# The second layer with its operands exchanged: token parts stationary, 384 weight columns moving, and one accumulator bank handed to attention

## The chip, the cores and the metric

The kernel runs on one core of a Trainium2 chip. The metric is the device time of one execution in microseconds. Three runs of the kernel before took 716.56, 717.89 and 721.01 us, so the median is 717.89 us.

## The reference

The program computes a delta-rule linear attention over 4 batches, 8 heads, 768 steps and 48 dimensions per head, and puts its output through a dense two-layer network with a softplus between the layers, all in float32. (The code calls the network a MoE, but there is one expert and no routing.)

```python
for t in range(S):                               # S = 768, per batch and head
    y[:, :, t] = np.einsum('bhd,bhde->bhe', q[:, :, t], state)
    v_old = np.einsum('bhde,bhd->bhe', state, k_n[:, :, t])
    state = state + bt * np.einsum('bhd,bhe->bhde', k_n[:, :, t], vt - v_old)
...
h = x @ w_in                                     # 3072 tokens x 384  ->  2048
g = np.maximum(h, 0.0) + np.log1p(np.exp(-np.abs(h)))
return (g @ w_out).astype(np.float32)            # 3072 x 2048  ->  384
```

## The kernel before

Time is cut into 12 chunks of 64 steps. With 4 batches, a chunk is 256 tokens of the network. Attention runs chunk by chunk: `gram` forms the products of the keys, `invert` solves small triangular systems column by column on VectorE (lines 214 and 220, once for each pair of chunks), `cross`, `seq_a` and `seq_b` carry the state through the chunk (TensorE matmuls of 32 to 64 columns, with PSUM results copied out by ScalarE and VectorE). It writes the chunk's output `x` as two float32r parts, high and low.

The network works on a chunk's 256 tokens. `DFF` = 2048 hidden rows are 16 tiles `f` of 128, taken two at a time, so there are 12 x 8 = 96 groups. In a group:

- **First layer (L422)**: for each of the two `f`, 9 matmuls (3 row tiles times 3 terms of the high/low split) with the weights as the stationary operand (128x128) and 256 token columns moving, into the PSUM tile `ph`. That is 18 matmuls a group, 1728 in all.
- **Softplus**: ScalarE L426, L427, L428, VectorE L429, then VectorE L432 rounds to the high part `gh`, and GpSimd L433 makes the low part `gl`. `ph`, `a`, `gh` and `gl` have two buffers each.
- **Second layer (L406)**, in the inner function `outp`: for each `f`, 3 terms (high weights with `gh`, low weights with `gh`, high weights with `gl`) times 3 tiles `e` of 128 output columns. The weights are stationary and 256 tokens of `gh` or `gl` move. That is also 18 matmuls a group and 1728 in all. They accumulate over a whole chunk in `po`, a tile of three PSUM banks (one buffer), with the 384 outputs on partitions and the tokens along the row.

`outp` of a group is emitted after the first layer of the next group (`late`). At the end of a chunk ScalarE copies all of `po` to `ot` (L413) and SyncE stores it (L414); in the very last chunk the terms are sorted so that the three `gl` terms of each tile come last, and each 128-row tile is copied and stored by itself (L410, L411).

PSUM has eight banks: `ph` takes two, `po` three, and `ps_a`, which holds every PSUM tile of attention (`pa`), three.

Attention steps are emitted between network groups by `attend` with a target (`RATE`, `LEAD`, `FIRST`). Each engine then executes in a fixed order, which the framework's scheduler sets at build time; in the opening part the order of TensorE is written out by hand. Dependences are kept by tile: a matmul that writes one bank of `po` waits for an earlier copy that reads another bank of the same `po`.

Of the kernel before, what the change touches and what calls it, by code (L numbers as in the profile page):

```python
# [7 lines left out]
F32 = mybir.dt.float32  # L8
# [8 lines left out]
B, H, S, D = 4, 8, 768, 48  # L17
NT, DM, DFF = B * S, H * D, 2048
P = 128
C = 64                 # time steps per chunk  # L20
HB = 32                # half chunk
QB = 16                # quarter chunk
NS = S // C            # chunks
NP = B * H // 2        # head pairs, p = 4 * b + h // 2
NK = DM // P           # 128-row tiles of the model dimension
NF = DFF // P          # 128-row tiles of the hidden dimension
RATE, LEAD, FIRST = 1.15, 12, 3     # attention units per MoE group, their lead and head start
QW = C + D             # [Q^T | state] columns per pair
# Where a weight tile is staged: tiles that are not in use yet.
STAGE = "x2 x3 x1 w12 w13 w14 w15 x2 x3 x1 w12 w13 x2 x3 w15 x2".split()  # L30
N16 = 1                # pairs of chunks that are inverted from blocks of 16


@with_exitstack
def deltanet_moe(ctx, tc, kT, qT, kN, vN, beta, wts, out):
    nc = tc.nc
# [3 lines left out]
    two = E(tc.tile_pool(name="two", bufs=2))  # L40
    ps_h = E(tc.tile_pool(name="ps_h", bufs=2, space=PSUM))
    ps_o = E(tc.tile_pool(name="ps_o", bufs=1, space=PSUM))
    ps_a = E(tc.tile_pool(name="ps_a", bufs=3, space=PSUM))
    nc.scalar.preload_act_table_set("natural_log_exp_and_others")

# [1 line left out]
    # Of a pair of heads (a, b), a has its tokens on partitions 0-63 and its d rows on 64-111,  # L47
    # b its tokens on 64-127 and its d rows on 0-47.
    tk = [slice(ab * C, (ab + 1) * C) for ab in range(2)]
    lo = [slice(ab * C, ab * C + HB) for ab in range(2)]  # L50
    hi = [slice(ab * C + HB, (ab + 1) * C) for ab in range(2)]
# [2 lines left out]
    pad = [slice((1 - ab) * C + HB, (2 - ab) * C) for ab in range(2)]  # L54

    kts = [const.tile([P, NP, C], F32, name=f"kt{i}") for i in range(3)]
    # Per head and pair: [P^T | U] on the token rows, [Q^T | state] on the d rows.
    big = const.tile([P, 2 * NP * QW + 16], F32, name="big")
    bv = big[:, 0:2 * NP * QW].rearrange("p (h a c) -> p h a c", h=2, c=QW)
    # Per head and pair: K on the token rows, the identity on the d rows.  # L60
    ki = const.tile([P, 2, NP, D], F32, name="ki")
    Z = const.tile([P, HB, HB], F32, name="Z")
    maskL = const.tile([P, QB], F32, name="maskL")
# [114 lines left out]
            nc.scalar.copy(off[hi[ab]], pa[hi[ab]])  # L178

    def invert(u, cT, ncT):  # L180
        # Z = (1 + diag(c) L)^-1 diag(c) per block: row m starts from its diagonal, and each of its
        # columns j, once final, is carried to the columns before it.
        ltq = one.tile([P, HB, HB], F32, name="ltq")
        nc.vector.transpose(ltq.rearrange("p j i -> p i j"),
                            LTD[u].rearrange("p q i -> p i q"))
        n = QB if u < N16 else HB
        blocks = range(0, HB, n)
        for a in blocks:
            d = (slice(None), slice(a, a + n), slice(a, a + n))
            mask = nc.gpsimd.affine_select(  # L190
                out=Z[d], in_=ncT[:, a:a + n].unsqueeze(1).to_broadcast([P, n, n]),
                compare_op=ALU.is_gt, fill=0.0, base=0, pattern=[[1, n], [-1, n]],
                channel_multiplier=0)
            nc.vector.tensor_tensor(ltq[d], ltq[d], Z[d], op=ALU.mult)
            nc.vector.tensor_tensor(Z[d], ltq[d],
                                    cT[:, a:a + n].unsqueeze(2).to_broadcast([P, n, n]),
                                    op=ALU.mult)
        lds = []
        if u < N16:
            for j in range(2):  # L200
                ld = two.tile([P, NP, HB], F32, name="gh")
                nc.gpsimd.memset(ld[:, :, QB:], 0.0)
                nc.gpsimd.tensor_tensor(ld[:, :, 0:QB], LTD[u][:, j * NP:(j + 1) * NP, 0:QB],
                                        maskL.unsqueeze(1).to_broadcast([P, NP, QB]), op=ALU.mult)
                lds.append(ld)
        if u == 0:
            tmp = one.tile([P, HB, HB], F32, name="tx")
        else:
            tmp = one.tile([P, HB, HB], F32, name="work")
        nc.vector.tensor_copy(Z.rearrange("p a b -> p (a b)")[:, 0:HB * HB:HB + 1], cT)  # L210
        for j in range(n - 2, 0, -1):
            r = n - 1 - j
            for a in blocks:
                nc.vector.tensor_tensor(  # L214
                    tmp[:, a:a + r, 0:j],
                    Z[:, a + j + 1:a + n, a + j:a + j + 1].to_broadcast([P, r, j]),
                    ltq[:, a + j:a + j + 1, a:a + j].to_broadcast([P, r, j]), op=ALU.mult)
            for a in blocks:
                zj = Z[:, a + j + 1:a + n, a:a + j]
                nc.vector.tensor_tensor(zj, zj, tmp[:, a:a + r, 0:j], op=ALU.add)  # L220
        return mask, lds
# [6 lines left out]
                                   Z.rearrange("p c j -> p j c") if u < N16 else Z)  # L228

    def join(u, lds):  # L230
        # Blocks of 16 joined to blocks of 32: Z = D - D L D, D the inverted blocks of 16.
        td, tx = TD[u], TX[u]
        for j in range(2):
            w1 = two.tile([P, NP, QB], F32, name="gl")
# [127 lines left out]
            yield  # L362

    def weights(f):
        # float64 words to float32, then to float32r parts: 2^e (0 below float32's range) times
        # 1 + mantissa.
        st = one.tile([P, 4 * DM], I32, name=STAGE[f])
        nc.sync.dma_start(st, wts[f])
        words = st.rearrange("p (n w) -> p n w", w=2)
# [19 lines left out]
    def moe():  # L389
        n = B * C  # L390
        late = None
        for s in range(NS):
            xr = [[X[s][:, i, k].rearrange("p b t -> p (b t)") for k in range(NK)]
                  for i in range(2)]
            po = ps_o.tile([P, NK, 512], F32, name="po")

            def outp(f0, gh, gl, po=po, s=s):
                terms = [(f, i, e) for f in range(f0, f0 + 2) for i in range(3) for e in range(NK)]
                last = f0 + 2 == NF and s == NS - 1
                if last:  # L400
                    terms.sort(key=lambda t: (t[1] == 2, t[2]))
                if f0 + 2 == NF:
                    ot = two.tile([P, NK, n], F32, name="ex", bufs=3)
                for f, i, e in terms:
                    a, b = ((0, 0), (1, 0), (0, 1))[i]
                    nc.tensor.matmul(po[:, e, 0:n], W[f][:, a, DM + e * P:DM + (e + 1) * P],  # L406
                                     (gh, gl)[b][:, f - f0], start=(f == 0 and i == 0),
                                     stop=(f == NF - 1 and i == 2))
                    if last and f == NF - 1 and i == 2:
                        nc.scalar.copy(ot[:, e], po[:, e, 0:n])  # L410
                        nc.sync.dma_start(out[s, e], ot[:, e])  # L411
                if f0 + 2 == NF and not last:
                    nc.scalar.copy(ot, po[:, :, 0:n])  # L413
                    nc.sync.dma_start(out[s].rearrange("e p c -> p e c"), ot)  # L414

            for f0 in range(0, NF, 2):
                ph = ps_h.tile([P, 2, n], F32, name="ph")
# [104 lines left out]
            steps_done = s + 1  # L522

    def attend(steps, target):
        """Emits attention work, at least so many steps and up to a number of units."""
        nonlocal units
        while steps_done < NS and (steps_done < steps or units + 1 <= target):
            r = next(ag, None)
# [65 lines left out]
```

## Time and profile before

| | before |
|---|---|
| median of three runs | 717.89 us |
| span of the profiled execution | 718.2 us (the page gives no other time of it) |
| TensorE matmuls, busy | 633.2 us, 88% |
| TensorE weight loads, busy | 599.3 us, 83% |
| VectorE busy | 488.6 us, 68% |
| ScalarE busy | 365.7 us, 51% |
| GpSimd busy | 246.4 us, 34% |

How to read it: a matmul and its weight load are separate rows (PE and PEld) and overlap; a matmul's end is modelled, so the number that counts is the distance between the starts of two matmuls that follow each other. Plain float32 matmuls, as attention has them, appear as two records each, float32r ones, as the network has them, as one. The span stands 0.3 us above the median of the runs, so the profiled execution can be taken for a typical one.

### The profile page before, as it was taken

To read this page: it belongs to the slowest core of one execution; us is meant where nothing else is said; L and a number is where in the kernel's file an instruction comes from. 1 tells how busy PE (TensorE), PEld (TensorE's weight loads), DVE (VectorE), ACT (ScalarE), POOL (GpSimd) and SP (SyncE) were. 2 spreads that over 40 slices of the span, in tenths; PEclk is the share of its full clock that TensorE was granted. 3 is DMA by queue.
4 is the path that set the end of the run, shared out by engine and by line. 5 is a ranking of instruction groups with operands and counts; after the bars stand their busy time and mean duration, and the time that the engine had idled before them with its cause. 6 is when DMAs were issued, how large, how long until landed. Compare 5 with 4: busy or idle time off the path is not lost.

```text
span 718.2 us, 23130 instructions
## 1 busy us (share of the span) xinstructions
PE 633.2 (88%) x10176; PEld 599.3 (83%) x10176; DVE 488.6 (68%) x956; ACT 365.7 (51%) x667; POOL 246.4 (34%) x183
## 2 busy tenths in 40 slices
PE   4227566879999899998999999999999999999997
PEld 3226556778899799998899999999989999999997
DVE  3999999999789955699635998459992524222221
ACT  3537875465365344652445545456545454544443
POOL 5517776553241221521213323233222222232232
PEclk9999568899999999999999999999999999999999
DMA  9923431202213121220213111321202121000000
GB/s 229 321 77 98 112 116 42 67 24 57 68 47 79 46 57 50 65 56 24 60 42 92 47 35 46 79 69 36 68 24 57 46 38 43 2 13 23 1 23 23
DMA packets 36563, 44.83 MB, mean 62 GB/s; under 512 B 21616, under 2 KB 28656, under 8 KB 36464
## 3 DMA queue, kind: packets, MB, share of 16 engines
q1 hardware_dynamic: 36464, 43.36, 21.6%
q8 instruction: 80, 1.31, 0.8%
q14 instruction: 19, 0.16, 0.1%
HBM read 36.27 MB, written 4.72 MB: 57 GB/s over the span
## 4 chain that ended last, share of the span: by engine, by line
PE 50%; DVE 38%; issue 4%; DMA 3%; ACT 2%; POOL 2%; SPq 1%; DVEq 0%; POOLq 0%; ACTq 0%
PE po L406 21%; PE ph L422 19%; DVE Z L220 6%; DVE work L214 6%; DVE a L429 3%; PE pa L291 2%; DVE ex L378 2%; DVE ex L374 2%; DVE big L298 2%; DVE gh L432 2%; PE pa L336 2%; DMA x<-wts 2%; DVE big L295 2%; PE pa L324 1%; DVE x L383 1%
## 5 line engine op out<-in xcount | busy, mean ns | idle before, releaser
L422 PE MATMUL ph<-x,w 128*128 128x256 f32 x1728 | 238.8, 292 | 9.2 <-DVE a L429 7.2
L433 POOL TENSOR_TENSOR gl<-a,gh 128x512 fp32r<-128x512 f32 x96 | 128.0, 1334 | 345.5 <-DVE gh L432 297.2
L422 PEld LDWEIGHTS ph<-x,w 128*128 128x128 f32 x1728 | 222.7, 198 | 14.3 <-DVE a L429 7.7
L406 PE MATMUL po<-gh,w 128*128 128x256 f32 x1152 | 176.4, 290 | 8.2 <-DVE gh L432 6.8
L426 ACT ACTIVATE a<-ph 128x512 f32<-128x512 f32 x96 | 57.3, 597 | 216.4 <-PE ph L422 212.7
L429 DVE SCALAR_TENSOR_TENSOR a<-ph,a 128x512 f32<-128x512 f32 x96 | 66.0, 688 | 148.2 <-ACT a L428 147.7
L406 PEld LDWEIGHTS po<-gh,w 128*128 128x128 f32 x1152 | 152.5, 193 | 13.6 <-DVE gh L432 8.5
L406 PE MATMUL po<-gl,w 128*128 128x256 f32 x576 | 103.8, 289 | 3.8 <-POOL gl L433 2.2
L406 PEld LDWEIGHTS po<-gl,w 128*128 128x128 f32 x576 | 82.8, 192 | 7.9 <-POOL gl L433 5.4
L214 DVE TENSOR_TENSOR work<-Z,ltq 128x30 f32<-128x30 f32 (+9 forms) x150 | 64.4, 429 | 3.8
L220 DVE TENSOR_TENSOR Z<-Z,work 128x30 f32<-128x30 f32 (+9 forms) x150 | 63.9, 426 | 3.9
L427 ACT ACTIVATE a<-a 128x512 f32<-128x512 f32 x96 | 60.5, 630 | 2.9
L428 ACT ACTIVATE a<-a 128x512 f32<-128x512 f32 x96 | 60.6, 631 | 2.0
L432 DVE CAST gh<-a 128x512 fp32r<-128x512 f32 x96 | 47.9, 500 | 2.4
L295 DVE TENSOR_TENSOR big<-nv,pa 64x192 f32<-64x192 f32 x88 | 30.9, 351 | 18.3 <-PE pa L291 16.6
L291 PE MATMUL pa<-big,kt 48*64 48x112 f32 x704 | 41.6, 265 | 0.3 <-DVE big L298 0.3
L291 PEld LDWEIGHTS pa<-big,kt 48*64 48x64 f32 x704 | 35.0, 136 | 4.1 <-PE pa L291 0.5
L298 DVE TENSOR_TENSOR big<-pa,maskP 64x256 f32<-64x256 f32 x88 | 37.0, 421 | 1.4
L112 POOL TENSOR_TENSOR nv<-nv 128x768 f32<-128x768 f32 x10 | 15.3, 1526 | 43.4 <-DMA nv<-kN 43.4
L327 ACT COPY big<-pa 32x384 f32<-32x384 f32 x48 | 22.6, 471 | 11.1 <-PE pa L324 10.1
L336 PE MATMUL pa<-big 128*64 128x64 f32 x768 | 27.9, 230 | 0.2
L336 PEld LDWEIGHTS pa<-big 128*64 128x64 f32 x768 | 25.5, 143 | 2.6 <-ACT big L327 0.7
(103 smaller groups left out, 758.8 us busy)
## 6 DMA issues: line engine op xcount, KB each, us to landing
x<-wts SPq DMA_DIRECT2D x9, 768.0 KB, 4.4
w<-wts SPq DMA_DIRECT2D x7, 768.0 KB, 10.0
kt<-kT SPq DMA_DIRECT2D x24, 192.0 KB, 3.3
big<-qT SPq DMA_DIRECT2D x24, 192.0 KB, 4.0
ki<-kN SPq DMA_DIRECT2D x24, 192.0 KB, 3.3
nv<-vN SPq DMA_DIRECT2D x12, 384.0 KB, 3.1
nv<-kN SPq DMA_DIRECT2D x11, 384.0 KB, 3.1
out<-ex SPq DMA_DIRECT2D x11, 384.0 KB, 2.6
```

The source lines that it names most:

```text
L214: nc.vector.tensor_tensor(tmp[:, a:a + r, 0:j], Z[:, a + j + 1:a + n, a + j:a + j + 1].to_broadcast([P, r, j]), ltq[:, a + j:a + j + 1, a: ...
L220: nc.vector.tensor_tensor(zj, zj, tmp[:, a:a + r, 0:j], op=ALU.add)
L291: nc.tensor.matmul(pk[tk[ab], pp, :], kt[dr[ab], p, :], bv[dr[ab], ab, p, :], start=True, stop=True)
L336: nc.tensor.matmul(py[tk[ab], pp, :], big[:, at + C:at + 2 * C], big[:, at:at + C], start=True, stop=True)
L406: nc.tensor.matmul(po[:, e, 0:n], W[f][:, a, DM + e * P:DM + (e + 1) * P], (gh, gl)[b][:, f - f0], start=(f == 0 and i == 0), stop=(f == N ...
L422: nc.tensor.matmul(ph[:, f - f0], W[f][:, a, k * P:(k + 1) * P], xr[b][k], start=(c == 0), stop=(c == 3 * NK - 1))
L426: nc.scalar.activation(a, ph, AF.Abs)
L427: nc.scalar.activation(a, a, AF.Exp, scale=-1.0)
L428: nc.scalar.activation(a, a, AF.Ln, bias=1.0)
L429: nc.vector.scalar_tensor_tensor(a, ph, 0.0, a, op0=ALU.max, op1=ALU.add)
L432: nc.vector.tensor_copy(gh, a)
L433: nc.gpsimd.tensor_tensor(gl, a, gh, op=ALU.subtract)
```

## The change

Only the second layer is turned round. The 128-token slice of `gh` or `gl` is now the stationary operand, and all 384 output columns of the weights move. With two halves `h` of 128 tokens, a group has 2 x 3 x 2 = 12 matmuls of 384 columns in place of 18 of 256. `po` needs two banks in place of three, one for each half, and holds tokens on partitions and outputs along the row. The last group of every chunk sorts its terms by half, and each half is copied (128x384) and stored by itself: 24 copies and 24 stores in place of 11 + 3. The freed bank goes to `ps_a`, which gets four. The output array in memory has another shape to match. Comments were taken out too. The file lost four lines, so that L422 and L433 of before are L418 and L429 after the change, L406 becomes L405, L413 becomes L409.

```diff
-    ps_a = E(tc.tile_pool(name="ps_a", bufs=3, space=PSUM))
+    ps_a = E(tc.tile_pool(name="ps_a", bufs=4, space=PSUM))
...
-            po = ps_o.tile([P, NK, 512], F32, name="po")
+            po = ps_o.tile([P, 2, 512], F32, name="po")
 
             def outp(f0, gh, gl, po=po, s=s):
-                terms = [(f, i, e) for f in range(f0, f0 + 2) for i in range(3) for e in range(NK)]
-                last = f0 + 2 == NF and s == NS - 1
-                if last:
-                    terms.sort(key=lambda t: (t[1] == 2, t[2]))
+                terms = [(f, i, h) for f in range(f0, f0 + 2) for i in range(3) for h in range(2)]
                 if f0 + 2 == NF:
-                    ot = two.tile([P, NK, n], F32, name="ex", bufs=3)
-                for f, i, e in terms:
+                    terms.sort(key=lambda t: t[2])
+                    ot = two.tile([P, 2, DM], F32, name="ex", bufs=3)
+                for f, i, h in terms:
                     a, b = ((0, 0), (1, 0), (0, 1))[i]
-                    nc.tensor.matmul(po[:, e, 0:n], W[f][:, a, DM + e * P:DM + (e + 1) * P],
-                                     (gh, gl)[b][:, f - f0], start=(f == 0 and i == 0),
+                    nc.tensor.matmul(po[:, h, 0:DM], (gh, gl)[b][:, f - f0, h * P:(h + 1) * P],
+                                     W[f][:, a, DM:], start=(f == 0 and i == 0),
                                      stop=(f == NF - 1 and i == 2))
-                    if last and f == NF - 1 and i == 2:
-                        nc.scalar.copy(ot[:, e], po[:, e, 0:n])
-                        nc.sync.dma_start(out[s, e], ot[:, e])
-                if f0 + 2 == NF and not last:
-                    nc.scalar.copy(ot, po[:, :, 0:n])
-                    nc.sync.dma_start(out[s].rearrange("e p c -> p e c"), ot)
+                    if f == NF - 1 and i == 2:
+                        nc.scalar.copy(ot[:, h], po[:, h, 0:DM])
+                        nc.sync.dma_start(out[s, h], ot[:, h])
...
-    args.append(nc.dram_tensor("out", (NS, NK, P, B * C), F32, kind="ExternalOutput").ap())
+    args.append(nc.dram_tensor("out", (NS, 2, P, DM), F32, kind="ExternalOutput").ap())
```

The scheduler makes a new order from this on every engine. Three places on TensorE matter below. In their rows L406 and L422 are the second and the first layer before, L405 and L418 the same after the change.

**Place one, the end of the first network chunk.** Before, from the last first-layer matmuls that stand between the second layer's:

```order
L422 MATMUL ph<-x_1597,w_813 128x256 x4
L406 MATMUL po<-gh,w_967 128x256 x6
L422 MATMUL ph<-x_1597,w_813 128x256 x5
L406 MATMUL po<-gl,w_967 128x256 x3
L406 MATMUL po<-gh,w_981 128x256 x6
L406 MATMUL po<-gl,w_981 128x256 x3
L422 MATMUL ph<-x_1597,w_827 128x256 x9
L422 MATMUL ph<-x_1597,w_841 128x256 x9
```

After the change, the same place:

```order
L418 MATMUL ph<-x_1585,w_813 128x256 x7
L405 MATMUL po<-w_967,gh 128x384 x2
L418 MATMUL ph<-x_1585,w_813 128x256 x2
L405 MATMUL po<-w_967,gl 128x384
L405 MATMUL po<-w_981,gh 128x384 x2
L405 MATMUL po<-w_981,gl 128x384
L418 MATMUL ph<-x_1585,w_827 128x256 x9
L418 MATMUL ph<-x_1585,w_841 128x256 x9
L405 MATMUL po<-w_967,gh 128x384 x2
L405 MATMUL po<-w_967,gl 128x384
```

Before, the last group of the chunk (weights w_967 and w_981) is finished in one go, and a first-layer group follows. Now its first half is finished, a first-layer group (w_827, w_841) comes between, and then the second half, which has to wait for the copy of the first.

**Place two, a little later, where attention's `cross` (L261) and `seq_a` (L291) come.** Before:

```order
L261 MATMUL pa<-td,off 32x32 x32
L291 MATMUL pa<-big,kt_76 64x112 x16
L406 MATMUL po<-gh,w_799 128x256 x6
L422 MATMUL ph<-x_1597,w_855 128x256 x4
L291 MATMUL pa<-big,kt_76 64x112 x8
L406 MATMUL po<-gl,w_799 128x256
L291 MATMUL pa<-big,kt_76 64x112 x8
L406 MATMUL po<-gl,w_799 128x256 x2
L406 MATMUL po<-gh,w_813 128x256 x6
L406 MATMUL po<-gl,w_813 128x256 x3
```

After the change:

```order
L405 MATMUL po<-w_155,gh 128x384 x4
L405 MATMUL po<-w_155,gl 128x384 x2
L261 MATMUL pa<-td,off 32x32 x32
L291 MATMUL pa<-big,kt_76 64x112 x32
L405 MATMUL po<-w_799,gh 128x384 x4
L405 MATMUL po<-w_799,gl 128x384 x2
L405 MATMUL po<-w_813,gh 128x384 x4
L405 MATMUL po<-w_813,gl 128x384 x2
```

Before, `seq_a`'s 32 matmuls stand in three pieces between second-layer matmuls, and four first-layer ones stand among them. Now all 32, which fill four banks of `ps_a`, stand in one piece right behind `cross`, whose result holds one of the four.

**Place three, the end of the program.** Before, the last seven rows, of 48 second-layer matmuls that stand behind the last of L422:

```order
L406 MATMUL po<-gh,w_981 128x256 x2
L406 MATMUL po<-gl,w_967 128x256
L406 MATMUL po<-gl,w_981 128x256
L406 MATMUL po<-gl,w_967 128x256
L406 MATMUL po<-gl,w_981 128x256
L406 MATMUL po<-gl,w_967 128x256
L406 MATMUL po<-gl,w_981 128x256
```

After the change, all rows from the last first-layer matmuls on, without the last three:

```order
L418 MATMUL ph<-x_7970,w_981 128x256 x6
L405 MATMUL po<-w_939,gh 128x384 x4
L405 MATMUL po<-w_939,gl 128x384 x2
L405 MATMUL po<-w_953,gh 128x384 x4
L405 MATMUL po<-w_953,gl 128x384 x2
L405 MATMUL po<-w_967,gh 128x384 x2
L405 MATMUL po<-w_967,gl 128x384
L405 MATMUL po<-w_981,gh 128x384 x2
L405 MATMUL po<-w_981,gl 128x384
L405 MATMUL po<-w_967,gh 128x384 x2
```

Now 24 second-layer matmuls stand behind the last first-layer one. Of the last group's twelve, the third already needs `gl`; before, the twelve that need only `gh` all stood ahead of the six that need `gl`.

Over the whole program, TensorE changes between network and attention matmuls 211 times before and 233 times after the change.

More of the change, by code (lines that the diff above doesn't have):

```diff
@@ L591 @@
     r = _run(nc, [data], core_ids=[0])
-    o = r.results[0]["out"].reshape(NS, NK, P, B, C).transpose(3, 0, 4, 1, 2)
+    o = r.results[0]["out"].reshape(NS, B, C, DM).transpose(1, 0, 2, 3)
     return np.ascontiguousarray(o).reshape(NT, DM)
```

## The prediction

> **What bounds the kernel now.** I read the page first: the busy shares, the slices and the chain.
>
> ```profile
> PE 633.2 (88%) x10176; PEld 599.3 (83%) x10176; DVE 488.6 (68%) x956; ACT 365.7 (51%) x667; POOL 246.4 (34%) x183
> ...
> PE   4227566879999899998999999999999999999997
> ...
> DVE  3999999999789955699635998459992524222221
> ...
> PEclk9999568899999999999999999999999999999999
> ...
> PE 50%; DVE 38%; issue 4%; DMA 3%; ACT 2%; POOL 2%; SPq 1%; DVEq 0%; POOLq 0%; ACTq 0%
> ```
>
> A slice is 18 us. For the first nine or ten VectorE is full and TensorE is not; after that TensorE is full to the end, and VectorE comes back to nine tenths in some places. The chain says the same: half of it is TensorE, 38% VectorE. So I asked for stretches, cut where the inversions are (all engines first, then the second layer alone).
>
> ```profile
> core 0: us, PE busy (x) PEld busy (x) DVE busy (x) ACT busy (x) POOL busy (x), PEclk, DMA share, GB/s
> 107.00:171.00 64.00, 50.51 (x734) 45.93 (x733) 62.88 (x95) 35.17 (x58) 35.62 (x20) 0.88 0.16 47
> 208.00:251.00 43.00, 41.00 (x612) 38.02 (x612) 39.84 (x89) 20.98 (x40) 11.35 (x9) 1.00 0.20 52
> ...
> 485.00:528.00 43.00, 41.73 (x660) 39.18 (x658) 40.95 (x93) 22.73 (x46) 12.13 (x9) 1.00 0.16 43
> 528.00:634.00 106.00, 105.82 (x1550) 102.19 (x1551) 42.75 (x95) 52.23 (x100) 24.77 (x19) 1.00 0.15 37
> ```
>
> ```profile
> 0.00:171.00 171.00, 19.18 (x126) 17.05 (x126) 0.88 0.40 117
> 208.00:251.00 43.00, 15.64 (x112) 13.85 (x112) 1.00 0.20 52
> 302.00:346.00 44.00, 16.01 (x113) 14.11 (x114) 1.00 0.20 51
> 395.00:435.00 40.00, 15.71 (x113) 13.78 (x111) 1.00 0.17 47
> 485.00:528.00 43.00, 14.81 (x108) 13.39 (x108) 1.00 0.16 43
> ```
>
> There are three kinds of stretch. Up to 171 us VectorE sets the pace (62.88 of 64 us in the last part); 126 second-layer matmuls are there, 7 groups of 18. In four later stretches (the first and the last are shown) VectorE is at 93% (39.84 of 43) to 95% (40.95) and TensorE is not quite full; 112 + 113 + 113 + 108 = 446 matmuls, 24.8 groups. In the rest TensorE is as good as always busy (105.82 of 106): 1728 - 126 - 446 = 1156 matmuls, 64.2 groups. Only there is TensorE time certainly time of the kernel.
>
> **What one matmul of 384 columns costs.** The trace has none. It has 256 columns at full clock and at half the granted clock, here first-layer matmuls in rows without another's between (start, length of the row, count; the second row is from the stretch whose clock the third gives), and weight loads of several widths (mean ns behind the bar's first comma).
>
> ```profile
> 647.02 3.52 PE L422 MATMUL ph<-x,w 128*128 128x256 f32 x28
> ```
>
> ```profile
> 115.08 3.41 PE L422 MATMUL ph<-x,w 128*128 128x256 f32 x15
> ```
>
> ```profile
> 115.50:118.00 2.50, 2.50 (x13) 2.50 (x13) 0.50 0.03 7
> ```
>
> ```profile
> L422 PE MATMUL ph<-x,w x18: 323/415/420, 114.7 to 118.3; 128*128 128x256 f32 x18
> ```
>
> ```profile
> L422 PEld LDWEIGHTS ph<-x,w 128*128 128x128 f32 x1728 | 222.7, 198 | 14.3 <-DVE a L429 7.7 <-issue 1.6 <-DMA x<-x 1.3
> ...
> L149 PEld LDWEIGHTS pa<-kt 48*32 48x32 f32 x640 | 19.0, 110 | 8.1 <-issue 6.8 <-ACT off L155 0.2
> ```
>
> At half clock a matmul lasts 0.415 us, so the starts are (3.41 - 0.415) / 14 = 214 ns apart: 0.835 ns a column. At full clock they are (3.52 - 0.28) / 27 = 120 ns apart, with 0.28 for the last one's length (0.29 is the mean of L422 in the page's groups). Streaming at twice the half-clock rate would be 107 ns, so 13 of the 120 are something else. Loading 96 columns more takes 198 - 110 = 88 ns, 0.92 ns a column, so 128 stationary columns need about 117 ns beside a stream of 107. The load, I conclude, sets the 120, and at half clock, where the distance is twice 107 and no more, nothing stands on top of the stream. With 384 columns the stream is 160 ns, longer than the load. I take **162 ns**, 160 and a little for the hand-over. The bounds are 160 (nothing on top) and 180 (120 x 384 / 256: the 120 grow with the columns); between them lies 173 (13 ns added to every matmul). I choose the low end because the half-clock row shows no addition.
>
> The Trainium skill, "TensorE: Matmul & The Clock Gate", section "Back-to-back issue gap", gives N/2.4 + 2.5 ns between two matmuls at the full clock, for 256 columns an estimate of 109 ns. The trace's 120 is 11 more, so the formula alone doesn't hold here. Its estimate for 384 columns is 162.5 ns, with which the saving below would be 64.2 x 0.21 = 13.5 us.
>
> **The change part by part.**
>
> *Second layer.* A group was 18 x 120 = 2.16 us and becomes 12 x 162 = 1.94, so 0.216 saved. In the 64.2 groups of the full stretches that is **-13.9 us**. In the four VectorE stretches it could be up to 24.8 x 0.216 = 5.4 more; but what TensorE does sooner there it waits longer for, since `gh` comes from the engine that is at 95%. I take 0 and keep 5.4 as the bound. In the first 171 us: 0.
>
> *More changes between network and attention.* 233 - 211 = 22 in the order, 11 round trips. What one costs is seen in the chain, where all is dense:
>
> ```profile
> 553.20 2.34 PE po L406 x18
> 555.54 2.16 PE ph L422 x18
> 557.70 1.68 PE pa L291 x32
> ```
>
> ```profile
> 600.18 1.75 PE L291 MATMUL pa<-big,kt 48*64 48x112 f32 x32
> ```
>
> The second layer's 18 take 2.34 behind attention against 2.16 for the first layer's 18 behind network matmuls: 0.18 for going in. The 32 records of L291 take 1.68 in the chain, while their own pace is about (1.75 - 0.26) / 31 x 32 = 1.54 (0.26 is the length of one): 0.14 for coming out. 11 x 0.32 = **+3.5 us**. The bounds are 0 and twice that.
>
> *Four banks.* At place two `seq_a` fills its fourth bank only when ScalarE has emptied `cross`'s, and those two copies stand behind a group's three activations.
>
> ```profile
> L426 ACT ACTIVATE a<-ph 128x512 f32<-128x512 f32 x96 | 57.3, 597 | 216.4 <-PE ph L422 212.7 <-POOL nv L285 3.6
> L264 ACT ACTIVATE tx<-pa 32x512 f32<-32x512 f32 x24 | 14.0, 583 | 6.3 <-PE pa L261 3.7 <-DVE tx L227 2.3
> L413 ACT COPY ex<-po 128x768 f32<-128x768 f32 x11 | 8.8, 801 | 12.7 <-PE po L406 12.6
> ```
>
> Three activations of 0.6 and two copies of 0.58 are 3.0 us; 24 of the 32 records run meanwhile (1.26), so a wait of up to 1.7 us. Behind it come second-layer groups without first-layer ones between, so TensorE uses up its finished `gh` and `gl`. A new `gl` is there 4.8 us after its first-layer matmuls (worked out at the end, below), and 12 matmuls (1.94) and a step of attention (1.68) take 3.6 of them: a wait of 1.2, twice. That is some **+3.5 us** with a part of the first wait, between 0 and 7 (twice that). That attention can run further ahead elsewhere I cost at 0: TensorE is full there and its sum is the same.
>
> *End of a chunk.* The copies become 24 of about 0.48 us (between 0.37 for 256 and 0.80 for 768 columns), 11.5 us against 9.9 on ScalarE, which is busy 51%: 0. The second half waits for the first half's copy (the tile is one), and the next chunk's groups stand behind it on TensorE; but in the order a first-layer group of 2.16 us covers it (place one), except at the very end. If that cover were gone, 11 times 0.5 us would show. The stores are 24 in place of 14 on SyncE's queue. Each waits for its copy, the second some 2 us after the first, and behind it stand the moves of `x` (L347) and attention's loads; TensorE's waits from 170 us on are these now:
>
> ```profile
> PE po L406 <- DVE gh L432: 3.7, 3, 1.9
> PE po L406 <- POOL gl L433: 1.8, 5, 0.7
> PE po L406 <- DVE Z L220: 1.3, 1, 1.3
> PE ph L422 <- DMA x<-x: 1.1, 2, 0.7
> ```
>
> For the moves of `x` it is 1.1 us in two waits, and I add nothing; if every one of the 11 stores held a move up by 2 us, 22 us would be the bound, but the wait of 1.1 us for eleven moves shows how far ahead they run.
>
> *The end.*
>
> ```profile
> 707.42 5.37 PE po L406 x44
> ...
> 714.74 0.37 ACT ex L410
> ```
>
> ```profile
> 710.33 0.43 DVE L432 CAST gh<-a 128x512 fp32r<-128x512 f32 x1
> ...
> 710.92 1.29 POOL L433 TENSOR_TENSOR gl<-a,gh 128x512 fp32r<-128x512 f32 x1 [3.03 <-DVE gh L432]
> ```
>
> The last first-layer matmul ends where these 44 begin, at 707.42. `gh` is there 3.3 us later, `gl` 4.8, the last copy's end 7.7 (715.11). Before, 48 matmuls fill the time (5.8 us) and TensorE hardly waits. After, 24 (3.9 us) stand there: TensorE waits for `gh`, then for `gl` until 4.8, then 4 matmuls (0.65), copy of the first half (0.5 and 0.1 on the way), 6 matmuls and the drain (1.2), copy (0.5): 7.8. The stretch is as long, but holds 24 x 0.162 = 3.9 of TensorE's work and not 5.8, so **+2.0 us** stand before it that I had counted as saved.
>
> **Sum**: -13.9 + 3.5 + 3.5 + 2.0 = -4.9 us against a span of 718.2, which is the median of 717.89 within 0.3. So 713 us.
>
> **Rivals.**
> - *VectorE follows.* The stretches at 95% shrink too (-5.4), and the new waits do not come (-3.5): 704 us. For it: TensorE is at 95 and 97% in the two that are shown. Against it: two of the three largest waits above are for VectorE already, and 5 us would have to come out of the 5 to 7% in which VectorE idles there, some 10 us.
> - *A fixed addition.* 173 ns: a group is 2.08 us, 64.2 x 0.08 = -5.1, and +3.5 + 3.5 + 1.6 stay: 721.4 us. For it: 13 ns are there at full clock. Against: not at half.
> - *Slower: the moving operand's own rate.* If at full clock a column takes 120/256 = 0.47 ns, 12 matmuls of 180 are as long as 18 of 120, nothing is saved, and 3.5 + 3.5 + 1.5 are paid: 726.4 us. It decides from the matmul's distance: at 168 ns the 9 us of waits eat the gain (64.2 x 0.144 = 9.2), above it the kernel is slower. For it: only 256-column rows exist at full clock. Against: the weight load's own length explains the 120.
> - *The change doesn't do what it says*: excluded, the order has 1152 matmuls of 384 columns.
>
> **How the numbers follow.** Forecast 0.60 (707 to 718 by the bounds of its waits), VectorE follows 0.16, fixed addition 0.14, rate 0.10. The likeliest is 713. The range 703 to 724 leaves out the rate and half of the fast rival, under 2 in 10. Within 1% (7.2 us, about what a measurement of this kernel can tell): most of the forecast and the fixed addition, 0.64. Faster by over 1% (under 710.7): the fast rival and a fifth of the forecast, 0.28. Slower (over 725.1): 0.08.
>
> **What the profile after would show.** Step one is right if 12 second-layer matmuls in a row are about 1.95 us apart from the next, 162 ns each; 2.08 or 2.16 name the rivals. The changes cost what I say if the second layer behind attention takes 0.18 more than behind the first. The bank is right if TensorE waits some 2 us at L291 for L264 near 190 us, and the end if its last first-layer matmul stands 7.8 us before the last copy's end. If TensorE's waits from 170 us on, 8 us in the four rows above, stay at 8, the gain is larger and I was wrong there; if they pass 22, the prediction fails on the other side.

## The result and the profile after

The changed kernel takes 726.51 us (723.51 to 727.06) against 717.69 for the kernel before on the same chip: ratio 1.0109, interval 1.0079 to 1.0138. I had forecast 713 and a range of 703 to 724, so the prediction is wrong, on the slow side. A run takes 1.9 us more than the span of its profile (726.02 against 724.1), so before's first profile, from which I summed, stood at 720, over its median and not at it.

The page of the changed kernel, in the order in which I read before's (busy shares, 40 slices, granted clock, the chain by engine):

```profile
PE 640.7 (88%) x9600; PEld 594.8 (82%) x9600; DVE 491.2 (68%) x956; ACT 366.7 (51%) x677; POOL 246.0 (34%) x183
...
PE   4227657979989999998999999999999999999996
...
DVE  4999999999678955799546998349992524222221
...
PEclk9999677799989999999899999999999999999997
...
PE 49%; DVE 36%; issue 4%; DMA 4%; ACT 3%; POOL 2%; SPq 1%; POOLq 0%; DVEq 0%; ACTq 0%
...
L405 PE MATMUL po<-w,gh 128*128 128x384 f32 x768 | 181.2, 353 | 10.5 <-DVE gh L428 9.8
```

TensorE has 576 records fewer and is busy longer, 640.7 us for 633.2. The clock's row has dents that before's doesn't show (the 12th, 20th and last slices read 8, 8 and 7). The chain, where work is dense:

```profile
569.82 2.30 PE po L405 x12
572.13 2.15 PE ph L418 x18
574.27 1.48 PE pa L313 x64
575.75 2.28 PE po L405 x12
```

12 second-layer matmuls behind attention take 2.28 to 2.30 us, where 18 took 2.34. So a group behind attention saves 0.05, not 0.22. TensorE's waits from 170 us on:

```profile
PE po L405 <- DVE gh L428: 5.6, 5, 1.9
PE po L405 <- POOL gl L429: 4.9, 8, 1.9
PE pa L313 <- DVE big L295: 1.5, 1, 1.5
PE ph L418 <- DVE a L425: 0.7, 2, 0.5
PE po L405 <- ACT ex L409: 0.6, 1, 0.6
PE pa L291 <- ACT tx L264: 0.4, 1, 0.4
```

They sum to 13.7 us, between the 8 and the 22 that I had named as limits. The last row is the four-bank wait: 0.4 us, not 2. The program's end (chain, then a window with TensorE's busy time and the clock):

```profile
710.68 0.73 PE ph L418 x6
...
716.16 1.38 PE po L405 x4
717.53 0.02 issue
717.55 0.49 ACT ex L409
718.04 0.04 issue
718.09 2.30 PE po L405 x6
720.39 0.02 issue
720.41 0.48 ACT ex L409
```

```profile
712.00:724.00 12.00, 5.74 (x21) 4.09 (x19) 1.12 (x2) 2.32 (x5) 1.27 (x1) 0.69 0.09 33
```

The last matmuls run at half clock, 0.32 us each in the records. The last first-layer matmul ends at 711.41 and the last copy at 720.89: 9.5 us, not 7.8.

**Where the time goes.** I cut the program at four marks that every variant has: the last second-layer matmul of the 13th, 61st, 93rd and 96th group. The 61st comes right after the last inversion, the 96th is the last. Worked out from the traces' start times (us), with the end of the last inversion's L214 and L220 beside them; a row with a number such as e7 is an experiment below:

```
                               13th   61st   96th   13-61  61-93  93-96  last inversion ends
before, first profile         209.7  537.6  714.4  327.9  166.6   10.2   531.8
before, second profile (e12)  206.9  534.1  710.9  327.2  166.6   10.2   528.3
changed                       211.6  541.0  719.8  329.4  165.8   13.0   536.6
changed, again (e5)           212.7  542.2  720.6  329.5  165.8   12.6   535.8
360 columns (e9)              211.9  540.0  713.2  328.1  162.5   10.7   536.7
one copy, unsorted (e3)       214.6  544.2  719.4  329.6  164.7   10.5   539.2
one copy, sorted (e10)        214.9  542.1  718.1  327.1  164.7   11.3   537.1
end sorted as before (e4)     213.5  542.5  719.2  329.1  165.8   10.8   537.4
exchange alone (e7)           215.1  539.5  713.6  324.4  164.7    9.5   536.3
gl ahead (e17)                208.9  540.5  719.6  331.6  165.8   13.3   536.1
before, loads apart (e14)     214.1  531.9  709.3  317.8  167.2   10.2   521.0
exchange, loads apart (e13)   213.7  530.4  704.6  316.8  164.7    9.5   520.0
changed, loads apart (e15)    213.5  533.1  711.6  319.6  165.8   12.7   523.9
```

The changed kernel is 2 to 6 us late at the 13th group, loses some 2 more up to the 61st, gains 0.8 up to the 93rd, and loses 2.4 to 2.8 in the last three groups. Two profiles of the same kernel differ by 1 to 3 us at the 13th group and by 0.7 at most in the parts behind it, so those parts compare better than the marks themselves.

### The profile page after: what moved, and what is told of

Read it like the earlier page. It is cut to its first block, busy times and chain, and to the rows that moved or that the text cites. A ratio compares the mean times of both kernels' runs of the same rounds, so it can differ in the third digit from the quotient of the medians.

```text
span 724.1 us, 21983 instructions
## 1 busy us (share of the span) xinstructions
PE 640.7 (88%) x9600; PEld 594.8 (82%) x9600; DVE 491.2 (68%) x956; ACT 366.7 (51%) x677; POOL 246.0 (34%) x183
## 4 chain that ended last, share of the span: by engine, by line
PE 49%; DVE 36%; issue 4%; DMA 4%; ACT 3%; POOL 2%; SPq 1%; POOLq 0%; DVEq 0%; ACTq 0%
PE po L405 20%; PE ph L418 18%; DVE Z L220 6%; DVE work L214 6%; PE pa L291 3%; DVE a L425 3%; PE pa L336 3%; DVE ex L378 2%; DMA nv<-kN 2%; DVE gh L428 2%; DVE ex L374 2%; DVE big L298 2%; DVE big L295 2%; DMA x<-wts 1%; PE pa L358 1%
## 5 line engine op out<-in xcount | busy, mean ns | idle before, releaser
L418 PE MATMUL ph<-x,w 128*128 128x256 f32 x1728 | 240.6, 292 | 12.3 <-DVE a L425 9.6
L429 POOL TENSOR_TENSOR gl<-a,gh 128x512 fp32r<-128x512 f32 x96 | 127.8, 1331 | 339.8 <-DVE gh L428 291.8
L418 PEld LDWEIGHTS ph<-x,w 128*128 128x128 f32 x1728 | 227.1, 197 | 18.9 <-DVE a L425 10.9
L405 PE MATMUL po<-w,gh 128*128 128x384 f32 x768 | 181.2, 353 | 10.5 <-DVE gh L428 9.8
L422 ACT ACTIVATE a<-ph 128x512 f32<-128x512 f32 x96 | 57.4, 598 | 221.4 <-PE ph L418 215.1
L405 PEld LDWEIGHTS po<-w,gh 128*128 128x128 f32 x768 | 134.8, 194 | 17.1 <-DVE gh L428 11.9
L405 PE MATMUL po<-w,gl 128*128 128x384 f32 x384 | 107.5, 351 | 5.4 <-POOL gl L429 5.2
L405 PEld LDWEIGHTS po<-w,gl 128*128 128x128 f32 x384 | 70.0, 194 | 9.7 <-POOL gl L429 8.6
L220 DVE TENSOR_TENSOR Z<-Z,work 128x30 f32<-128x30 f32 (+9 forms) x150 | 68.3, 455 | 3.9
L214 DVE TENSOR_TENSOR work<-Z,ltq 128x30 f32<-128x30 f32 (+9 forms) x150 | 66.4, 443 | 3.8
L428 DVE CAST gh<-a 128x512 fp32r<-128x512 f32 x96 | 45.4, 473 | 5.6 <-PE po L405 3.2
L291 PE MATMUL pa<-big,kt 48*64 48x112 f32 x704 | 44.6, 271 | 0.4 <-ACT tx L264 0.4
L291 PEld LDWEIGHTS pa<-big,kt 48*64 48x64 f32 x704 | 37.4, 139 | 6.9 <-issue 4.3
```

Source lines behind the costliest of these rows:

```text
L214: nc.vector.tensor_tensor(tmp[:, a:a + r, 0:j], Z[:, a + j + 1:a + n, a + j:a + j + 1].to_broadcast([P, r, j]), ltq[:, a + j:a + j + 1, a: ...
L291: nc.tensor.matmul(pk[tk[ab], pp, :], kt[dr[ab], p, :], bv[dr[ab], ab, p, :], start=True, stop=True)
L405: nc.tensor.matmul(po[:, h, 0:DM], (gh, gl)[b][:, f - f0, h * P:(h + 1) * P], W[f][:, a, DM:], start=(f == 0 and i == 0), stop=(f == NF - ...
L418: nc.tensor.matmul(ph[:, f - f0], W[f][:, a, k * P:(k + 1) * P], xr[b][k], start=(c == 0), stop=(c == 3 * NK - 1))
L422: nc.scalar.activation(a, ph, AF.Abs)
L428: nc.vector.tensor_copy(gh, a)
```

## The experiments

**e1, the distance by itself.** A program of its own that leaves the whole computation out: rows of 64 matmuls, TensorE alone.

> Matmuls alone, no attention and no network: 64 in a row of each kind, every one with a weight load of its own, after 192 that warm the clock. The output is zeros, so only the distances between matmuls count. float32r with 128 stationary columns and 256, 320, 384, 512 moving; 64 stationary with 256 and 384; 32 stationary with 384; the same 128 columns again and again with 384; bfloat16 with 256 and 384; all 384 into one bank. Theory A (a fixed addition of 13 ns to the stream): 120, 146, 173, 227 ns for the four widths, and the same 13 with 64 or 32 stationary columns. Theory B (the stationary side: the addition belongs to the load of 128 float32 columns): 13 ns with 128 stationary columns, half of it or less with 64, little with 32, and little in bfloat16, whose load is smaller. Theory C (the moving operand's rate, 0.47 ns a column): 120, 150, 180, 240 ns. The prediction's own figure was 162 for 384.

Its timeline (start, length, line, shape, count). From one row's start to the next is 64 distances:

```profile
37.97 7.84 PE L40 MATMUL pa<-wr 128*128 128x256 f32 x64
45.65 9.55 PE L42 MATMUL pa<-wr 128*128 128x320 f32 x64
55.04 11.26 PE L44 MATMUL pa<-wr 128*128 128x384 f32 x64
66.14 14.71 PE L46 MATMUL pa<-wr 128*128 128x512 f32 x64
80.69 7.42 PE L48 MATMUL pa<-wr 128*64 128x256 f32 x64
87.95 11.25 PE L50 MATMUL pa<-wr 128*64 128x384 f32 x64
99.03 11.27 PE L52 MATMUL pa<-wr 128*32 128x384 f32 x64
110.14 11.26 PE L54 MATMUL pa<-wr 128*128 128x384 f32 x64
121.24 7.16 PE L56 MATMUL pa<-wb 128*128 128x256 bf16 x64
128.24 10.56 PE L58 MATMUL pa<-wb 128*128 128x384 bf16 x64
```

(45.65 - 37.97) / 64 = 120 ns for 256 columns, 147 for 320, 173.4 for 384, 227 for 512: the columns at 2.4 per ns and 13.3 ns on top. With 64 or 32 stationary columns, or the same weights 64 times (L54), 384 columns still take 173 to 174. So at 384 columns the weight load does not set the distance, as I had taken it. At 256 it isn't as plain: with 64 stationary columns (L48) a matmul takes 113 ns, so half of the 13 is gone, as theory B had it. What the 13 ns are stays open. In bf16 256 columns take 109.

**e9, the distance in place.** 360 of the 384 columns, which leaves 24 outputs out.

```diff
-  nc.tensor.matmul(po[:, h, 0:DM], ..., W[f][:, a, DM:],
+  nc.tensor.matmul(po[:, h, 0:360], ..., W[f][:, a, DM:DM + 360],
```

> The changed kernel with 360 of the 384 output columns computed (the last 24 are left out), so that a second-layer matmul should stand 360 / 2.4 + 13.3 = 163.3 ns from the next: the 162 of my forecast within a nanosecond; 237 changes between network and attention by the order, against 233. If the distance was the step that failed, with its gain in the 64.2 full groups: 727 - 64.2 x 12 x 0.0103 = 719 us (717.5 to 720.5), ratio 1.001; if it counts in all 96 groups: 715, ratio 0.996. If all my other terms had been right it would be 713 to 715. Rival, that waits and not the distance set the pace: 724 or more, ratio above 1.007.

718.48 us, ratio 1.0011 (0.9997 to 1.0025), as the distance theory expected. Had a matmul stood 163 ns from the next, the change would have been neutral and not a gain. The table qualifies it. Between the 61st and 93rd group 32 x 12 x 0.0103 = 4.0 us were to be had, and 3.3 came (162.5 for 165.8). The last three groups gain 2.3, more than the 0.4 of their matmuls. Between the 13th and 61st, where 5.9 were to be had, only 1.3 came; TensorE's waits for `gl` from 170 us on are 8.5 us here, for 4.9 in the changed kernel.

**e2, the fourth bank**: `ps_a` with `bufs=3`, otherwise as changed.

> The changed kernel with three banks for attention, as before the change, and one bank of PSUM unused. Theory 'the fourth bank costs': the order of attention goes back to pieces, the waits near 205 to 210 us go, and the time falls by 3 to 4 us against the changed kernel, to about 722. Theory 'the bank is nothing': the same as the changed kernel within 1.5 us, 725 to 728, since the matmuls' sum is the same and the order still has many more changes between network and attention than the kernel before.

726.26 us, 1.0118 (1.0097 to 1.0139), as the second theory had it: the bank does nothing to the time either way. The changed kernel's waits of 1.5 and 1.9 us near 204 and 207 us are gone here, and the 13th group still comes at 212.0.

**e3 and e10, the chunk ends.** One copy and one store per chunk but the last; e3 also drops the sorting there, e10 keeps it.

```diff
-                    terms.sort(key=lambda t: t[2])            # only e3: sort where s == NS - 1
-                    if f == NF - 1 and i == 2:
+                    if s == NS - 1 and f == NF - 1 and i == 2:
                         nc.scalar.copy(ot[:, h], po[:, h, 0:DM])
...
+                if f0 + 2 == NF and s < NS - 1:
+                    nc.scalar.copy(ot, po[:, :, 0:DM])
```

> The changed kernel, but a chunk's last group is not sorted by half, and the accumulator is copied and stored in one piece at the end of the chunk, except in the last chunk. Theory 'the split end of a chunk costs' (it cuts the second layer's last group in two with other work between, so that there are more changes between network and attention, and the second half waits for a copy): about 10 changes fewer at 0.3 us and no waits for the first copy, 3 us faster than the changed kernel, about 723. Theory 'it is covered': the same within 1.5 us.

> The changed kernel with the terms of a chunk's last group sorted by half, as in it, but with one copy and one store for both halves in the first eleven chunks (the last chunk as in the changed kernel). 223 changes between network and attention by the order, as with the unsorted single copy, against 233 in the changed kernel. If the split copies and stores, or the order that they bring, cost the 4 us: 722.5 us (721 to 724), ratio 1.006. If the sorting costs them: 727, ratio 1.011.

e3: 722.17 us, 1.0051 (1.0033 to 1.0070). e10: 724.24, 1.0094 (1.0071 to 1.0116), so neither theory of e10 is met. Without sorting and split copies the kernel is about 4 us faster. e10's interval overlaps the changed kernel's, so how the 4 divide is not settled; the order moves as well (223 changes between network and attention for 233). The table shows how far from the edit the gain can lie: between the 61st and 93rd group both versions gain 1.1 us, but the last three groups gain 2.5 in e3 and 1.7 in e10, although their source there is the changed kernel's. Only the order differs: 32 second-layer matmuls stand behind the last first-layer one, for 24.

**e4 and e5, the end of the program.** e4 sorts the last chunk's `gl` terms last as before; e5 is the changed kernel again.

> The changed kernel with one edit: in the very last group the terms that need the low part come last, as in the kernel before. Theory 'the end's waits bring the half clock': TensorE stops once and not twice ahead of its last 12 matmuls, for about 2 us less; the last 12 or most of them run at full clock, 174 ns and not 320; in sum 1.5 to 2.5 us faster than the changed kernel. Theory 'waits alone': only the order of the last 12 changes, about 0.7 us (four matmuls of 174 ns) faster, too little to see in the times, but visible in the trace.

> The changed kernel itself once more, so that the variants beside it have a reference on the same chip. Both theories: 726.4 us (725 to 728), ratio 1.011. In the profile the slow clock windows behind TensorE's waits near 206, 339, 530 and 716 us should come back if the waits cause them (theory: waits of about 2 us drop the clock, so the places are fixed by the program); if they are a matter of chance of one execution, the places differ.

e4: 724.98 us, 1.0093 (1.0073 to 1.0112). e5: 727.2, 1.0107 (1.0078 to 1.0136). In time the difference is not resolved. In the table it shows: e4's last three groups take 10.8 us, for 13.0 and 12.6, all else behind the 13th group is the same within 0.4, and at the end no half-clock window starts before its last matmul. In e5 the half-clock windows come again at 210, 340, 531 and 718 us, within 2 us of the first profile's (208, 341, 532, 717), so here the program fixes their places. Before's two profiles have one such window between 170 us and the end, and it stands at 347 us in one and at 336 in the other.

**e6, the clock.** Extra matmuls in the free bank ahead of three groups where TensorE had waited; they ran at 340, 445 and 716 us.

```diff
+    FILL = {(3, 14): 12, (5, 12): 10, (11, 14): 14}
...
+    for k in range(FILL.get((s, f0), 0)):
+        nc.tensor.matmul(pf[:, 0:n], W[f0][:, 0, 0:P], xr[0][0], start=True, stop=True)
```

> Three attention banks; in the fourth, which nothing else uses, 12, 10 and 14 extra matmuls of 256 columns (36 x 0.12 = 4.3 us, results unused) stand ahead of three second-layer groups: those of the last first-layer pair of chunks 3 and 11 and of the pair before it in chunk 5, where TensorE waited 1.5 to 2 us for gh and the clock then dropped. Theory that such waits drop the clock and that this costs: the windows of half clock behind these places go (5 to 6 us of TensorE time in the changed kernel), the extra matmuls lie in the waits, and the time is 722 us (720 to 724), ratio 1.005. Rival, that the windows come whatever TensorE does: they stay, and the time is 726 to 730, the extra matmuls coming on top.

Windows of e2, which it is built on, and then of e6 (clock behind the brackets):

```profile
338.00:352.00 14.00, 11.74 (x138) 10.60 (x138) 11.70 (x25) 6.46 (x13) 4.19 (x3) 0.76 0.26 71
712.00:724.00 12.00, 7.34 (x30) 5.69 (x29) 1.12 (x2) 2.82 (x5) 1.27 (x1) 0.71 0.09 33
```

```profile
338.00:352.00 14.00, 12.11 (x136) 10.43 (x136) 13.21 (x31) 6.52 (x12) 4.25 (x3) 1.00 0.30 85
712.00:724.00 12.00, 7.99 (x49) 7.02 (x48) 1.12 (x2) 2.82 (x5) 2.01 (x2) 1.00 0.10 34
```

Where the waits at 340 and 716 us are filled the windows behind them go. (e2's wait at 444 had none behind it.) The one near 533, with no filling, stays, and one near 255 is new. The time hardly moves: 725.44, 1.0094 (1.0068 to 1.0120), overlapping e2. The expected 4 us were not there.

**e7, the exchange alone**: three banks, one unsorted copy per chunk, the end as before.

> The exchange of operands with three attention banks, one copy and one store per chunk as before the change, and the last chunk's gl terms last as before. What is left of the change is the exchange alone. If the parts add (4 us for the chunk ends, 1 to 1.5 for the end, 0 for the bank): 721 us (719.5 to 723), ratio 1.004. If a wait that one part removes comes back at the next place: 724 us, ratio 1.008. If the exchange alone were the gain that I predicted: below 714.

722.62 us, 1.0054 (1.0033 to 1.0075), in the range for parts that add. But e3 alone has the same time, and e4's share is not resolved, so whether they add stays open. By the table it gains on before 2.7 us behind the 61st group (1.9 up to the 93rd), some 3 between the 13th and 61st, and loses 5 to 8 by the 13th. Its profile is of its fastest run (719.87), so that loss may be larger in the others. The place shows in TensorE's row for 182 to 216 us, before's second profile first, then e7:

```profile
182.00:216.00 34.00, 33.95 (x676) 1.00 0.21 59
```

```profile
182.00:216.00 34.00, 31.12 (x595) 0.90 0.16 49
```

**e8 and e11, the rate.** `RATE` 1.19 for 1.15, in e7's kernel and in before.

> As the exchange alone with three banks, one copy per chunk and the end sorted, with RATE 1.19 for 1.15, so that attention is emitted a little sooner against the network's groups: fewer changes between network and attention (205 by the program's order, against 233 in the changed kernel and 211 before it). If the changes cost 0.33 us for each entry and exit and the waits stay as they are, 28 changes fewer than in the changed kernel give 4.6 us: 717 us (715 to 719), ratio 0.999. If the rate only moves the waits about: as with 1.15, 721 us. Under 714 it would beat both kernels.

> The kernel before with RATE 1.19 for 1.15 and nothing else: 209 changes between network and attention against 211. If the gain of the same edit in the exchanged kernel (722.6 to 716.7) came from its fewer changes (205 against 219), there is nothing to gain here: 718 us (717 to 720), ratio 1.000. If the rate itself helps: 713 to 714, ratio 0.993, and the exchange is then slower at either rate.

e8: 716.73 us, 0.9981 (0.9964 to 0.9997), where fewer changes were to put it. e11: 724.88, 1.0105 (1.0086 to 1.0125), slower with 209 changes for 211, which neither theory had; so the number of changes does not explain e8. At 1.15 the exchange alone is 4 us slower than before, at 1.19 it is 8 us faster than before at that rate. So at this one parameter's two values the order that the scheduler makes weighs more than the exchange itself.

**e12 to e15, the key loads.** The profile of before again, then an edit to three kernels: `nv` has one buffer, and each pair of chunks loads two blocks of keys and two of values through it. The second key load goes to `ltq`.

```diff
-        ka = one.tile([P, NP, D], F32, name="td" if s == 1 else "nv")
+        ka = one.tile([P, NP, D], F32, name="td" if s == 1 else "ltq" if s % 2 and s > 3 else "nv")
```

> The kernel before once more, for a second profile of it. Theory: TensorE's waits from 170 us on are 9 to 11 us again, none of over 1 us near 206 us, one slow clock window near 347 us behind a wait of 2 us, and span 715 to 719. If the waits near 206 us in the changed kernel are chance of an execution (a late transfer), they may stand here too.

> The exchange alone (three banks, one copy per chunk, end sorted as before), with the key rows of chunks 5, 7, 9 and 11 loaded into the tile ltq in place of nv, so that these loads, and that of vN behind them, don't wait for one another's use of nv. If the lost 8 us between 180 and 215 us come from GpSimd waiting at nv with gl behind it: 716.5 us (715 to 719), ratio 0.998, and the 12th group's last second-layer matmul at 207 to 210 us in place of 215. If the loss has another cause: 722.5, ratio 1.005.

> The kernel before with the same edit. There gl stands between the two multiplications of nv on GpSimd and TensorE waits for neither, so little is to be had: 717 us (715.5 to 718.5), ratio 0.999. If the loads delay every version alike: 712 to 714, ratio 0.993.

> The changed kernel with the same edit. It waits 3.5 us near 206 and 209 us for gl and gh behind nv, and its clock drops to half for 6.8 us behind that. If nv is the cause: 722 us (720 to 724), ratio 1.006. If not: 727, ratio 1.011.

e12's one run took 716.38 us, its span 714.6 (just under the expected 715), with no wait over 1 us near 206. e13: 714.13, 0.9944 (0.9918 to 0.9969). e14: 715.36, 0.9960 (0.9942 to 0.9977). e15: 717.65, 0.9990 (0.9975 to 1.0005). The edit gives the exchanged kernels 8.5 and 9 us, before 2.9. All three are faster than the theory's ranges. So the loads cost more than I had thought, but not at the place that I had named: the 13th group comes at 213.5 to 214 in all three, in before's case 4 to 7 us later than without the edit. GpSimd's timeline, changed kernel, then e13 (`Z<-ncT` opens the third inversion, once the norms are there):

```profile
195.37 1.47 POOL L112 TENSOR_TENSOR nv<-nv 128x768 f32<-128x768 f32 x1 [9.62 <-DMA nv<-kN]
...
200.83 1.47 POOL L112 TENSOR_TENSOR nv<-nv 128x768 f32<-128x768 f32 x1 [2.74 <-DMA nv<-kN]
206.43 1.48 POOL L285 TENSOR_TENSOR nv<-nv,nn 128x768 f32<-128x768 f32 x1 [4.13 <-DVE r L124]
207.87 1.27 POOL L429 TENSOR_TENSOR gl<-a,gh 128x512 fp32r<-128x512 f32 x1
209.25 1.27 POOL L190 TENSOR_SCALAR_AFFINE_SELECT Z<-ncT 128x1024 f32<-128x1024 f32 x1
```

```profile
194.44 1.47 POOL L112 TENSOR_TENSOR nv<-nv 128x768 f32<-128x768 f32 x1 [7.54 <-DMA nv<-kN]
200.25 1.47 POOL L285 TENSOR_TENSOR nv<-nv,nn 128x768 f32<-128x768 f32 x1 [4.34 <-DMA nv<-vN]
201.83 1.38 POOL L190 TENSOR_SCALAR_AFFINE_SELECT Z<-ncT 128x1024 f32<-128x1024 f32 x1
```

With the loads apart that inversion opens at 201.8, for 209.3 in the changed kernel, 209.9 in e7 and 209.3 and 207.2 in before; the last one ends 16 us sooner in e13, 12 to 13 in e15 and 7 to 11 in e14 (table). The stretch from the 13th to the 61st group shrinks by 7.6 us in e13, with the same TensorE work (the same 1440 matmuls of the network, 3508 records of attention for 3510), and by 9 to 10 in the other two. That much of its length hung on this chain and not on TensorE's matmuls.

**e17, one place on GpSimd.** In the changed kernel L285's multiplication is issued behind the `gl` that stands behind it above, as in before.

```diff
+        with tc.issue_after(GL[-6].ins) if s == 3 else nullcontext():
             nc.gpsimd.tensor_tensor(nV, nV, NN[s]...
```

> The changed kernel with one dependence more: chunk 3's multiplication of nv (L285) is issued on GpSimd behind the gl that stands ahead of it in before. GpSimd's order in that stretch is then before's; TensorE's differs from the changed kernel's in 19 rows, and it has 227 changes between network and attention for 233. If the order of these two is the early loss: the 13th group at 207 to 209 us in place of 212, and 722.5 us (721 to 724), ratio 1.006. If not: 212 us, and 726 to 727, ratio 1.011.

The 13th group comes at 208.9 as expected, and the time stays: 727.63, 1.0133 (1.0105 to 1.0161). TensorE's waits from 245 to 255 us, changed kernel and e17:

```profile
PE po L405 <- DVE gh L428: 0.6, 1, 0.6
```

```profile
PE po L408 <- DVE gh L431: 2.4, 1, 2.4
```

What is won at 209 is waited for at 250, and the 61st group comes at 540.5, as in the changed kernel (541.0). So winning back the loss up to the 13th group does not make this kernel faster.

**e16 and e18, a version below both**: e13's kernel at `RATE` 1.19 and 1.17.

> The exchange alone at RATE 1.19 (716.7 without the edit, ratio 0.998) with the same edit; 207 changes between network and attention by the order, against 205. It has gl behind the second nv multiplication too. If nv costs it some 3 us: 713.5 us (712 to 715), ratio 0.994, under both kernels. If not: 716.7.

> The exchange alone with the key loads apart, at RATE 1.17: 209 changes between network and attention by the order, against 219 at 1.15 (714.1) and 207 at 1.19 (713.1). If the number of changes orders them: 713.3 us (712 to 715), ratio 0.993. If the sequence that happens to come out decides, anything between 710 and 720.

713.01 us, 0.9929 (0.9905 to 0.9953), and 712.70, 0.9928 (0.9898 to 0.9957). Both beat both kernels, with the exchange and two small edits together; nothing is resolved between the two rates. How much of it is the exchange is not shown: with the loads apart at 1.15 the intervals of e13 and e14 (before) overlap, and before was not run at the other rates with the loads apart.

## Why the prediction was wrong

- **The 162 ns: the step that failed first.** The distance is 173.4 (e1), the "fixed addition" rival's. From one distance at full clock and one at half I had read the 13 ns as the weight load, which would hide under 384 columns; e1 shows them there at 384 too, with a quarter of the weights and with the same ones. The term of -13.9 becomes 64.2 x 0.079 = -5.1. That is 8.8 of the 13.5 us between forecast and result, and e9, with 163 ns in place, is 7 (by the ratios) to 8 us faster than the changed kernel. The Trainium skill, "TensorE: Matmul & The Clock Gate", section "Back-to-back issue gap", gives N/2.4 + 2.5 ns for an isolated matmul; e1's bf16 row agrees (109 by both for 256 columns), the float32r rows, 11 higher, do not.
- **The 64.2 groups: sure for half of them.** I counted a saving in every stretch in which TensorE was full. Behind the last inversion it comes: 32 groups x 0.079 (2.16 - 12 x 0.1734) = 2.5 us, and the exchange alone gains 1.9 there. Between the 13th and 61st group, where 48 x 0.079 = 3.8 us were to be had, the pairs differ: 2.8 to 3.5 at 1.15 (e7), 2.6 at 1.19 (e8's 328.7 for e11's 331.3), 1.1 with the loads apart (e13 and e14). Moving one load is worth 7.6 to 10 us there. So a nearly full TensorE between two inversions was not the only bound. That the next inversion starts from loads and norms is read from GpSimd's rows at one inversion.
- **More changes of work, +3.5**: entering behaved as I said (12 matmuls at 173.4 are 2.08, and take 0.20 to 0.22 more; I had 0.18). Their sum was not isolated, and e11 is slower with fewer of them.
- **Four banks, +3.5: not there.** The wait is 0.4 us, and e2's time is the same. I had misread a row: a plain float32 matmul leaves two records, so the 24 matmuls that run during `cross`'s copies are 48 records and take 2.5 us, not 1.26. Of the 3.0 us of activations and copies that leaves 0.5 to wait, not 1.7. The changed kernel's timeline:

```profile
183.54 2.52 PE L291 MATMUL pa<-big,kt 48*64 48x112 f32 x48
186.45 0.98 PE L291 MATMUL pa<-big,kt 48*64 48x112 f32 x16 [0.40 <-ACT tx L264]
```

- **Chunk ends, 0: wrong.** e3 is 4 us faster without them. The cover that I had counted on held: TensorE waits for a copy of `po` once, 0.6 us, at the program's end. What I had not looked at is what sorting and two copies do to the order around them, down to the program's end.
- **The end: too small.** The last three groups take 13.0 us against 10.2 in before, where I had a stretch as long as before. Waits of 1.40 and 0.99 came as drawn. The half clock behind them I had not priced: eight of the last twelve matmuls run in it, at about 320 in place of 173 ns, some 1.2 us.
- **The rivals.** "Fixed addition" had the right distance and gave 721.4; with the bank's 3.5 taken out and the chunk ends' 4 put in it gives 722, some 4.5 below the result. "Rate" had about the right time for a wrong reason: 384 columns take 173 ns and not 180. "VectorE follows" is refuted: the time is 726.5 and not 704, and TensorE's waits grew.

What stays open: what the 13 ns are, whether the parts add, how sorting and copies share their 4 us, and why the exchange alone loses 5 to 8 us by the 13th group at this `RATE`. Each edit also moves the scheduler's order, and no run keeps that fixed.

## What to carry to other kernels

Before a saving per instruction is multiplied, measure the instruction alone at the size it will have: one width gives no way to tell a fixed part from a rate. An engine that is busy but for a few waits is not proof that it is the bound; follow what starts the next long chain (here a single-buffered load), and give that chain its own buffer first. And where a scheduler orders the program, a parameter set for the old kernel can outweigh the change: compare both at more than one setting.

## What the runs showed of the hardware

float32r matmuls stood columns / 2.4 + 13.3 ns apart at full clock with 128 stationary columns (120, 147, 173, 227 ns for 256, 320, 384, 512). With 64 or 32 stationary columns 384 moving ones still took 173 to 174, but with 64 stationary 256 took 113 and not 120. bf16 ones stood 109 apart at 256. At half clock 384 columns took 320 ns, with nothing on top. In the changed kernel's two profiles the waits of TensorE near 206, 337, 529 and 715 us, of 0.8 to 2.1 us each, were followed within 4 us by windows of half clock, mostly of 3.4 or 6.8 us. They went where other matmuls filled the wait (e6). Not every such wait has one: before's of 1.5 us near 248 had none.
